# Fused linear attention and gated feed-forward layer: all row tails in the last block, batch 2's attention later in block 1, and half of batch 0's k^T v ahead of q's third turns

## The chip, the cores and the metric

The kernel runs on one core of a Trainium2 chip (trn2). The metric is the device time of one execution in microseconds (us); smaller is better. Five engines work on a core: PE (TensorE: matmuls and transposes by matmul, with a separate queue view PEld for its weight loads), DVE (VectorE), ACT (ScalarE), POOL (GpSimd) and SP (SyncE, which here only issues DMAs). POOL issues DMAs too.

## The reference

For 8 batches, 8 heads, 576 rows and a head size of 64, the attention is linear, with a cosine weight on the position; its output, with the heads side by side, is the input of a two-layer network:

```python
r = np.maximum(x, 0.0); phi(x) = np.concatenate([r * cos_w, r * sin_w], axis=-1)   # x: q or k
kv  = np.einsum('bhsf,bhsd->bhfd', k_p, v)
z   = np.sum(k_p, axis=2)
num = np.einsum('bhsf,bhfd->bhsd', q_p, kv)
den = np.einsum('bhsf,bhf->bhs', q_p, z)[..., None] + 1e-06
x   = (num / den).transpose(0, 2, 1, 3).reshape(4608, 512)
h   = x @ w_in                       # 512 x 2048
out = (h * sigmoid(1.702 * h)) @ w_out   # 2048 x 512
```

Inputs and output are float32; inside, matmuls take bf16 and add up in float32.

## The kernel before, in words

The order of all work is written out by hand: each engine runs its instructions in the order in which the program names them, and waits only for what it reads or overwrites. There is one block for each of the 8 batches. A block does the feed-forward layer of its batch and, in between, the attention of the next batch.

**Attention of a batch.** `trig` (lines 142 and 140) makes the weighted k (`kr`, nine slices of 64 rows, a cosine and a sine half each) on DVE, or on ACT with `act=True`. `vcopy` (lines 161 and 163) casts v to `vt`. For q there are two ways. In batches 0 and 1 `trig` makes nine slices `qn0`, `qturn_pe` (line 171) turns two slices at a time on PE and `qevac` (lines 179 and 181) copies them to `qT`. In batches 2 to 7 `trig_q` (line 155) and `qturn_dma` (line 189) do it in five chunks, the turn by a DMA that SP issues. `kv_mm` (line 207) is k^T v, 18 matmuls for each of four head pairs; `kv_evac` (line 212) copies it out of PSUM on DVE. `num_mm(c)` (line 230) is numerator and denominator of chunk c, that is 128 rows (chunk 4 has 64, the tail), `num_div` (lines 236, 238, 254) divides on DVE into `xn`. Then `xn` has to be turned: in batches 0 and 1 on PE (`xturn_mm`, line 272) with a copy on ACT (`xturn_evac`, line 279), in later batches by DMA (`xturn_dma`, line 285). `den_early` (line 244) makes the denominators of batch 0's first chunk ahead of its k^T v.

**Feed-forward.** The turned x of a batch has 512 columns, chunks 0 to 3, and a tail of 64 columns, chunk 4. `mm1(b, fc)` is four matmuls of 512 columns (line 295) for one of sixteen groups of 128 hidden units, with a Gelu on ACT (line 300). `mm2(b, t, lo, hi)` (line 345) is the second layer for row tile t of 128 rows over hidden groups lo to hi; when it is through, ACT copies it out (line 349), and a DMA stores it (line 352: POOL's queue, in the last block SP's).

**Tails.** Those of batches 0 and 1 are computed in their own blocks: `mm1_tail` (line 322) does 32 matmuls of 64 columns at a time, twice in a block, and a joint row tile `t == 4` of both batches goes through `mm2` in block 1. The tails of batches 2 to 7 wait in `xt` (384 columns); in the last block `mm1_tails` (line 313) does them with 16 x 4 matmuls of 384 columns, and three row tiles, 5 to 7, go through `mm2`.

**Order around the change.** At the start, batch 0: k is weighted, `ksum` makes z, q's slices are weighted on DVE, ACT and POOL as they land, PE turns them in pairs with some matmuls on a zero tile between them (`idle`, line 358), then come the two halves of k^T v with v from `vb`, which POOL's queue loads in two halves (line 132), and the first numerators. `start_block` (blocks 0 and 1) begins the first layer chunk by chunk, as x's chunks are turned. From block 1 on, DVE makes `trig_q`, `trig` and `vcopy` for the next batch while PE does the first layer; then PE does k^T v, and puts the numerators of the five chunks between half row tiles of the second layer. Behind the turns of x, SP issues the loads of k and v of the batch after (lines 562 to 564).

Of the kernel before, what the change touches and what calls it, by code (L numbers as in the profile page):

```python
# [19 lines left out]
def kernel(  # L20
# [9 lines left out]
    nc = tc.nc  # L30
# [80 lines left out]
    def w_in_of(kc, fc):  # L111
        return w_in_v[fc // 4][:, kc, fc % 4, :]
# [10 lines left out]
    def load_win(g):  # L123
        nc.gpsimd.dma_start(out=w_in_sb[g], in_=win_r[:, :, ts(g, 512)])
# [42 lines left out]
    def qturn_pe(c, home=None):  # L167
        tp = pmm.tile([128, 2, NI, 128], BF16, name="mm") if home is None else home
        for j in range(2 * c, min(2 * c + 2, NS)):
            for i in range(NI):  # L170
                nc.tensor.transpose(tp[:, j % 2, i], qn0[:, j, i, :], ident)  # L171
        tps[c] = tp
# [29 lines left out]
    def kv_mm(i0, i1, rhs, col, n):  # L202
        for i in range(i0, i1):
            for j in range(NS):
                for hh in range(2):
                    r = slice(hh * 64, hh * 64 + 64)
                    nc.tensor.matmul(st["kv", i][:, hh, ds(col, n)], kr[r, j, i, :], rhs(r, i, j),  # L207
                                     start=(j == 0), stop=(j == NS - 1))

    def kv_evac(i0, i1, n=65):  # L210
        o = st["kvs"][:, :, i0:i1, 0:n]
        nc.vector.tensor_copy(o, st["ps", i0].rearrange("p hh (i e) -> p hh i e", e=65)[:, :, :, 0:n])  # L212
# [13 lines left out]
    def num_mm(c):  # L226
        ps = pat.tile([128, 2, 512], F32, name="at")
        for h in range(H):
            i, hh = divmod(h, 2)
            nc.tensor.matmul(ps[:, h // 4, ds((h % 4) * 65, 65)], qT[:, h, ts(c, 128)],  # L230
                             st["kvs"][:, hh, i, 0:65], start=True, stop=True)
        nums[c] = [ps]
# [15 lines left out]
    def num_div(c, inv=None):  # L248
        ps = nums[c][0]
        pv = ps[:, :, 0:260].rearrange("p a (h e) -> p a h e", h=4)  # L250
        if inv is None:
            inv = inv_of(pv[:, :, :, 64])
        xn = small.tile([128, 2, 4, 64], BF16, name="xn", bufs=4)
        nc.vector.tensor_tensor(xn, pv[:, :, :, 0:64],  # L254
                                inv.unsqueeze(3).to_broadcast([128, 2, 4, 64]), op=MUL)
        nums[c].append(xn)

    x = {}

    TB = 2  # L260
    NT = (B - TB) * 64
    xt = one.tile([128, KC, NT], BF16, name="xt")

    def x_open(b):
        x[b] = xpool.tile([128, KC, S], BF16, name="xT")

    def xturn_mm(c):
        ps, xn = nums[c]
        xv = xn.rearrange("p a h e -> p (a h e)")
        for kc in range(KC):  # L270
            o = ps[:, kc // 2, ds(264 + (kc % 2) * 64, 64)].bitcast(BF16)
            nc.tensor.transpose(o, xv[:, ts(kc, 128)], ident)  # L272

    def xturn_evac(b, c):
        ps = nums.pop(c)[0]
        n = 128 if c < 4 else 64
        i = ps[:, :, 264:392].bitcast(BF16).rearrange("p a (k t) -> p a k t", k=2)[:, :, :, 0:n]
        o = x[b][:, :, c * 128:c * 128 + n].rearrange("p (a k) t -> p a k t", a=2)
        nc.scalar.activation(o, i, AF.Copy)  # L279

    def xturn_dma(b, c):
        xn = nums.pop(c)[1]
        n = 128 if c < 4 else 64
        o = xt[:, :, ts(b - TB, 64)] if c == 4 and b >= TB else x[b][:, :, c * 128:c * 128 + n]
        nc.sync.dma_start_transpose(out=o, in_=xn[0:n].rearrange("p a h e -> p (a h e)"))


    gT = {}
# [15 lines left out]
        mm1_part(b, fc, 0, MT)  # L304
        gelu(fc)

    gt = {}
    gl_t = one.tile([128, FC, NT], BF16, name="gl_t")

    def mm1_tails(fc):  # L310
# [2 lines left out]
            nc.tensor.matmul(hps, w_in_of(kc, fc), xt[:, kc, :], start=(kc == 0), stop=(kc == KC - 1))  # L313
        nc.scalar.activation(gl_t[:, fc, :], hps, AF.Gelu_apprx_sigmoid)  # L314

    def mm1_tail(b, half):
        if half == 0 and b % 2 == 0:
            gt[0] = gpool.tile([128, FC, 128], BF16, name="gtail", bufs=2)
        hps = pmm.tile([128, 8, 64], F32, name="mm")
        for f in range(8):  # L320
            for kc in range(KC):
                nc.tensor.matmul(hps[:, f], w_in_of(kc, half * 8 + f), x[b][:, kc, MT:S],  # L322
                                 start=(kc == 0), stop=(kc == KC - 1))
        nc.scalar.activation(gt[0][:, ts(half, 8), ts(b % 2, 64)], hps, AF.Gelu_apprx_sigmoid)

    yp = {}
    out_j = [out[b * S:b * S + S].rearrange("(p j) d -> j p d", j=NS) for b in range(2)]

    def rows(b, t):

        if t == 4:
            return [(64 * u, 64, out_j[u][NS - 1]) for u in range(2)]
        if t > 4:
            return [(64 * u, 64, out[(w + 1) * S - 64:(w + 1) * S])
                    for u, w in enumerate((TB + 2 * (t - 5), TB + 2 * (t - 5) + 1))]
        if b < 2:
            return [(64 * u, 64, out_j[b][2 * t + u]) for u in range(2)]
        return [(0, 128, out[b * S:b * S + 512].rearrange("(p c) d -> c p d", c=4)[t])]

    def mm2(b, t, lo, hi, c0=0, c1=d_model):  # L340
        if lo == 0:
            yp[t, c0] = pmm.tile([128, d_model], F32, name="mm")
        for fc in range(lo, hi):
            w = gT[fc][:, ts(t, 128)] if t < 4 else gt[0][:, fc, :] if t == 4 else gl_t[:, fc, ts(t - 5, 128)]
            nc.tensor.matmul(yp[t, c0][:, c0:c1], w, w_out_sb[:, fc, c0:c1],  # L345
                             start=(fc == 0), stop=(fc == FC - 1))
        if hi == FC:
            ysb = ypool.tile([128, d_model], F32, name="ysb")
            nc.scalar.activation(ysb[:, c0:c1], yp[t, c0][:, c0:c1], AF.Identity)  # L349
            for p0, n, dst in rows(b, t):  # L350
                eng = nc.sync if b == B - 1 else nc.gpsimd
                eng.dma_start(out=dst[:, c0:c1], in_=ysb[p0:p0 + n, c0:c1])  # L352
# [14 lines left out]
    def start_block(b, opened=False):  # L367

        if not opened:
            xturn_mm(0)  # L370
            xturn_evac(b, 0)
            num_mm(2)
            num_div(2)
            xturn_mm(1)
            xturn_evac(b, 1)
        for c in range(4):
            for fc in range(4):
                mm1_part(b, fc, c * 128, c * 128 + 128)
            if c == 0:
                num_mm(3)  # L380
                num_div(3)
                xturn_mm(2)
                xturn_evac(b, 2)
            if c == 1:
                num_mm(4)
                num_div(4)
                xturn_mm(3)
                xturn_evac(b, 3)
        for fc in range(4):
            gelu(fc)  # L390
        xturn_mm(4)
        mm1(b, 4)
        xturn_evac(b, 4)


    w = idle(12)
# [27 lines left out]
    nc.gpsimd.tensor_copy(gate[0:1, 1:2], vb[0:1, 3, 0:1])  # L424
    load_win(2)
    load_win(3)
    qturn_pe(2)
    for j in (6, 7):
        trig(qn0, qf0, j, act=True)
    qevac(0)  # L430
    qevac(1)
    qevac(2, act=True)
    kv_mm(0, 2, vb_rhs, 0, 64)
    inv0 = den_early(0)
    kv_evac(0, 2, 64)
    kv_mm(2, 4, vb_rhs, 0, 64)
# [22 lines left out]
        trig(kr, kf, j)  # L459
    for fc in range(5, FC):  # L460
        mm1(0, fc)
    mm1_tail(0, 0)
    mm1_tail(0, 1)
    for j in range(5):
        trig(qn0, qf0, j)
    for j in range(5, NS):
# [50 lines left out]
    for b in range(1, B):  # L517
        nb = b + 1 if b + 1 < B else None
        f0 = 5 if b == 1 else 0
        for fc in range(f0, FC):  # L520
            if nb is not None and fc == f0:
                for c in range(5):
                    trig_q(c)
                    qturn_dma(c)
                if nb + 1 < B:
                    load_q(nb + 1)
            if nb is not None and fc == f0 + 1:
                for j in range(NS):
                    trig(kr, kf, j)
                vcopy(0, 4)  # L530
            mm1(b, fc)
        if b < TB:
            mm1_tail(b, 0)
            mm1_tail(b, 1)
        if nb is None:
            for fc in range(FC):
                mm1_tails(fc)
            for t in (5, 6, 7):
                mm2(b, t, 0, FC)
            for t in range(3):  # L540
                mm2(b, t, 0, FC)
            mm2(b, 3, 0, FC, 0, 256)
            mm2(b, 3, 0, FC, 256, 512)
            continue
        x_open(nb)
        kv_open()
        kv_mm(0, 4, vt_rhs, 0, 65)
        kv_evac(0, 4)
        if b == 1:
            mm2(b, 4, 0, FC)  # L550
        for t in range(4):
            mm2(b, t, 0, 8)
            if t < 3:
                num_mm(2 * t)
                num_div(2 * t)
                xturn_dma(nb, 2 * t)
            mm2(b, t, 8, 16)
            if t < 2:
                num_mm(2 * t + 1)
                num_div(2 * t + 1)  # L560
                xturn_dma(nb, 2 * t + 1)
        if nb + 1 < B:
            load(kf, k, nb + 1, nc.sync)
            load(vf, v, nb + 1, nc.sync)
# [30 lines left out]
```

## Time and profile before

| | us |
|---|---|
| median of 3 runs | 293.15 (293.08 to 293.31) |
| the profiled execution, its own time | 293.47 |
| its span (first to last instruction) | 291.8 |
| PE busy | 286.0, 98% |
| DVE busy | 126.6, 43% |
| ACT busy | 130.4, 45% |
| PE's granted clock | 1.0 |

A profile page gives the busy time of each engine, the chain of work that ended last (followed back from the last instruction: at each step to what released it, or to the instruction before it on its engine) and groups of instructions by line. "PE at L207 x72" is 72 PE instructions of line 207 that write the tile "at". Timelines give start, length, engine, line and operation, and in brackets the idle time of the engine before it and what ended it. A waiting engine costs time only if others on the chain wait for it.

### The profile page before, as it was taken

The page shows a single profiled execution, that of the slowest core. Times are in us where ns is not written, and L with a number is a line of the kernel's source. Part 1 is how long each engine was busy: PE and PEld are TensorE (multiplying, and loading weights), DVE is VectorE, ACT ScalarE, POOL GpSimd, SP SyncE. Part 2 cuts the span into 40 slices and gives each one's busy share as a digit, 9 for nine tenths or more (in the row PEclk, how much of TensorE's full clock was granted, in tenths as well). Part 3 has the DMA queues.
Part 4 walks back from the last instruction along what each step waited for, and adds up shares of the span by engine and source line. Part 5 has one row for each costly group of instructions (what it writes and reads, how often), then busy time and mean ns, then how long its engine had stood idle before and what let it go on. Part 6 is the DMA issues. An engine that isn't in the chain of part 4 may idle for free.

```text
span 291.8 us, 6048 instructions
## 1 busy us (share of the span) xinstructions
PE 286.0 (98%) x2467; PEld 160.1 (55%) x2467; DVE 126.6 (43%) x364; ACT 130.4 (45%) x229; POOL 37.2 (13%) x70
## 2 busy tenths in 40 slices
PE   7999999999999999999999999999999999999995
PEld 3785656857545555555545554555455545565444
DVE  4864524791274636482658256625662420000000
ACT  7857743674115721472146313641265116773111
POOL 6650041400222001100110011001100010000000
PEclk9999999999999999999999999999999999999999
DMA  7999999595269966896579747995696341000322
GB/s 248 243 213 291 372 267 334 144 159 165 60 132 328 233 175 132 261 290 181 144 225 312 197 121 192 309 216 129 166 327 129 76 115 38 1 0 10 85 88 72
DMA packets 67227, 52.36 MB, mean 179 GB/s; under 512 B 47392, under 2 KB 57376, under 8 KB 67200
## 3 DMA queue, kind: packets, MB, share of 16 engines
q1 hardware_dynamic: 59824, 32.52, 44.5%
q0 software_dynamic: 7376, 19.47, 23.2%
q8 instruction: 19, 0.31, 0.4%
q14 instruction: 8, 0.07, 0.1%
HBM read 36.70 MB, written 9.44 MB: 158 GB/s over the span
## 4 chain that ended last, share of the span: by engine, by line
PE 95%; DMA 2%; DVE 1%; SPq 0%; ACT 0%; issue 0%; ACTq 0%
PE mm L345 43%; PE mm L295 38%; PE mm L313 4%; PE at L230 3%; PE at L207 3%; DMA qf<-in_q_dram 2%; PE mm L322 1%; PE at L272 1%; PE at L171 1%; DVE qn L142 1%; PE mm L171 0%; SPq L62 0%; ACT xT L279 0%; SPq L63 0%; PE mm L358 0%
## 5 line engine op out<-in xcount | busy, mean ns | idle before, releaser
L345 PE MATMUL mm<-w_out_sb,g 128*128 128x512 bf16 (+1 forms) x528 | 117.7, 372 | 0.0
L295 PE MATMUL mm<-xT,w_in 128*128 128x512 bf16 (+1 forms) x608 | 113.2, 345 | 0.0
L300 ACT ACTIVATE g<-mm 128x512 bf16<-128x512 f32 x128 | 75.7, 599 | 31.8 <-PE mm L295 31.8
L295 PEld LDWEIGHTS <-w_in 128*128 128x128 bf16 x608 | 62.0, 114 | 49.1
L345 PEld LDWEIGHTS <-g 128*128 128x128 bf16 x528 | 48.7, 98 | 49.5
L349 ACT ACTIVATE ysb<-mm 128x512 f32<-128x512 f32 (+1 forms) x37 | 21.7, 586 | 111.4 <-PE mm L345 111.4
L352 POOL DMA_DIRECT2D out_dram<-ysb x38 | 20.7, 547 | 177.1 <-ACT ysb L349 177.0
L142 DVE TENSOR_SCALAR kr<-kf,cosw 128x256 bf16<-128x256 f32 x68 | 23.7, 349 | 30.2 <-DMA kf<-in_k_dram 30.2
L254 DVE TENSOR_TENSOR xn<-at,inv 128x512 bf16<-128x512 f32 x40 | 27.7, 691 | 1.7 <-PE at L230 0.4
L142 DVE TENSOR_SCALAR kr<-kf,sinw 128x256 bf16<-128x256 f32 x68 | 23.9, 351 | 0.0
L236 DVE TENSOR_SCALAR den<-at 128x8 f32<-128x8 f32 x39 | 6.5, 166 | 36.5 <-PE at L230 36.5
L230 PEld LDWEIGHTS <-qT 128*128 128x128 bf16 x320 | 14.6, 97 | 8.1 <-issue 0.8
L212 DVE CAST kvs<-at 128x520 bf16<-128x520 f32 (+1 forms) x9 | 5.7, 635 | 29.1 <-PE at L207 29.1
L230 PE MATMUL at<-kvs,qT 128*128 128x65 bf16 x320 | 15.9, 193 | 0.7 <-ACT xT L279 0.7
L155 DVE TENSOR_SCALAR qn<-qf,sinw 128x512 bf16<-128x512 f32 (+1 forms) x30 | 14.3, 478 | 0.0
L155 DVE TENSOR_SCALAR qn<-qf,cosw 128x512 bf16<-128x512 f32 (+1 forms) x30 | 14.3, 477 | 0.0
L313 PE MATMUL mm<-xt,w_in 128*128 128x384 bf16 x64 | 10.6, 326 | 0.0
L345 PE MATMUL mm<-w_out_sb,gl_t 128*128 128x512 bf16 x48 | 10.5, 379 | 0.0
L207 PEld LDWEIGHTS <-kr 64*128 64x128 bf16 x576 | 9.2, 94 | 2.3 <-issue 2.0
L358 PE MATMUL mm<-warm 128*128 128x512 bf16 x23 | 8.6, 494 | 1.2 <-DVE warm L76 1.2
L313 PEld LDWEIGHTS <-w_in 128*128 128x128 bf16 x64 | 7.2, 113 | 3.3
L314 ACT ACTIVATE gl_t<-mm 128x384 bf16<-128x384 f32 x16 | 7.9, 491 | 2.4 <-PE mm L313 2.4
(68 smaller groups left out, 126.4 us busy)
## 6 DMA issues: line engine op xcount, KB each, us to landing
kf<-in_k_dram SPq DMA_DIRECT2D x5, 1152.0 KB, 6.7
vf<-in_v_dram SPq DMA_DIRECT2D x5, 1152.0 KB, 9.7
qf<-in_q_dram SPq DMA_DIRECT2D x5, 1024.0 KB, 6.1
out_dram<-ysb POOLq DMA_DIRECT2D x20, 256.0 KB, 2.6
kf<-in_k_dram POOLq DMA_DIRECT2D x2, 1152.0 KB, 10.6
vf<-in_v_dram POOLq DMA_DIRECT2D x2, 1152.0 KB, 14.4
out_dram<-ysb POOLq DMA_DIRECT2D x18, 128.0 KB, 3.1
w_in<-in_moe_w_in_dram POOLq DMA_DIRECT2D x4, 512.0 KB, 9.3
```

What stands on the lines that cost most here:

```text
L142: eng.tensor_scalar(o, i, 0.0, w[:, j:j + 1], op0=MAX, op1=MUL)
L155: nc.vector.tensor_scalar(o, i, 0.0, sc, op0=MAX, op1=MUL)
L207: nc.tensor.matmul(st["kv", i][:, hh, ds(col, n)], kr[r, j, i, :], rhs(r, i, j), start=(j == 0), stop=(j == NS - 1))
L230: nc.tensor.matmul(ps[:, h // 4, ds((h % 4) * 65, 65)], qT[:, h, ts(c, 128)], st["kvs"][:, hh, i, 0:65], start=True, stop=True)
L254: nc.vector.tensor_tensor(xn, pv[:, :, :, 0:64], inv.unsqueeze(3).to_broadcast([128, 2, 4, 64]), op=MUL)
L295: nc.tensor.matmul(hp[fc][:, t0:t1], w_in_of(kc, fc), x[b][:, kc, t0:t1], start=(kc == 0), stop=(kc == KC - 1))
L300: nc.scalar.activation(g, hp.pop(fc), AF.Gelu_apprx_sigmoid)
L313: nc.tensor.matmul(hps, w_in_of(kc, fc), xt[:, kc, :], start=(kc == 0), stop=(kc == KC - 1))
L345: nc.tensor.matmul(yp[t, c0][:, c0:c1], w, w_out_sb[:, fc, c0:c1], start=(fc == 0), stop=(fc == FC - 1))
L349: nc.scalar.activation(ysb[:, c0:c1], yp[t, c0][:, c0:c1], AF.Identity)
L352: eng.dma_start(out=dst[:, c0:c1], in_=ysb[p0:p0 + n, c0:c1])
L358: nc.tensor.matmul(w, warm[:, 0:128], warm, start=True, stop=True)
```

## The change

1. The tails of batches 0 and 1 join `xt`, which has 512 columns now (`NT = B * 64`); `mm1_tail` is gone, `mm1_tails` works on 512 columns, and four row tiles, 4 to 7, go through `mm2` in the last block. The tail chunk of batches 0 and 1 is turned by DMA (`xturn_dma(b, 4)`) and no longer on PE.
2. `start_block` has another order of its last first-layer parts: three hidden groups of chunk 2, two of chunk 3, the fourth of chunk 2, the other two of chunk 3.
3. In block 1, four of the nine k slices of batch 2 and half of its v copy go to ACT, between and behind the Gelus. k^T v and all that follows of batch 2's attention stand half a row tile of the second layer later (`lag`). In the blocks from 2 on, the rewritten loop gives the order of before.
4. In batch 0, `kv_mm(0, 2)` stands ahead of `qturn_pe(2)` and no longer behind it.

```diff
--- before.py
+++ after.py
@@ -257,12 +257,14 @@
 
     x = {}
 
-    TB = 2
-    NT = (B - TB) * 64
+    NT = B * 64
     xt = one.tile([128, KC, NT], BF16, name="xt")
 
     def x_open(b):
-        x[b] = xpool.tile([128, KC, S], BF16, name="xT")
+        x[b] = xpool.tile([128, KC, MT], BF16, name="xT")
+
+    def x_of(b, c):
+        return xt[:, :, ts(b, 64)] if c == 4 else x[b][:, :, ts(c, 128)]
 
     def xturn_mm(c):
         ps, xn = nums[c]
@@ -273,16 +275,14 @@
 
     def xturn_evac(b, c):
         ps = nums.pop(c)[0]
-        n = 128 if c < 4 else 64
-        i = ps[:, :, 264:392].bitcast(BF16).rearrange("p a (k t) -> p a k t", k=2)[:, :, :, 0:n]
-        o = x[b][:, :, c * 128:c * 128 + n].rearrange("p (a k) t -> p a k t", a=2)
+        i = ps[:, :, 264:392].bitcast(BF16).rearrange("p a (k t) -> p a k t", k=2)
+        o = x_of(b, c).rearrange("p (a k) t -> p a k t", a=2)
         nc.scalar.activation(o, i, AF.Copy)
 
     def xturn_dma(b, c):
         xn = nums.pop(c)[1]
         n = 128 if c < 4 else 64
-        o = xt[:, :, ts(b - TB, 64)] if c == 4 and b >= TB else x[b][:, :, c * 128:c * 128 + n]
-        nc.sync.dma_start_transpose(out=o, in_=xn[0:n].rearrange("p a h e -> p (a h e)"))
+        nc.sync.dma_start_transpose(out=x_of(b, c), in_=xn[0:n].rearrange("p a h e -> p (a h e)"))
 
 
     gT = {}
@@ -304,7 +304,6 @@
         mm1_part(b, fc, 0, MT)
         gelu(fc)
 
-    gt = {}
     gl_t = one.tile([128, FC, NT], BF16, name="gl_t")
 
     def mm1_tails(fc):
@@ -313,26 +312,14 @@
             nc.tensor.matmul(hps, w_in_of(kc, fc), xt[:, kc, :], start=(kc == 0), stop=(kc == KC - 1))
         nc.scalar.activation(gl_t[:, fc, :], hps, AF.Gelu_apprx_sigmoid)
 
-    def mm1_tail(b, half):
-        if half == 0 and b % 2 == 0:
-            gt[0] = gpool.tile([128, FC, 128], BF16, name="gtail", bufs=2)
-        hps = pmm.tile([128, 8, 64], F32, name="mm")
-        for f in range(8):
-            for kc in range(KC):
-                nc.tensor.matmul(hps[:, f], w_in_of(kc, half * 8 + f), x[b][:, kc, MT:S],
-                                 start=(kc == 0), stop=(kc == KC - 1))
-        nc.scalar.activation(gt[0][:, ts(half, 8), ts(b % 2, 64)], hps, AF.Gelu_apprx_sigmoid)
-
     yp = {}
     out_j = [out[b * S:b * S + S].rearrange("(p j) d -> j p d", j=NS) for b in range(2)]
 
     def rows(b, t):
 
-        if t == 4:
-            return [(64 * u, 64, out_j[u][NS - 1]) for u in range(2)]
-        if t > 4:
-            return [(64 * u, 64, out[(w + 1) * S - 64:(w + 1) * S])
-                    for u, w in enumerate((TB + 2 * (t - 5), TB + 2 * (t - 5) + 1))]
+        if t >= 4:
+            return [(64 * u, 64, out_j[w][NS - 1] if w < 2 else out[(w + 1) * S - 64:(w + 1) * S])
+                    for u, w in enumerate((2 * (t - 4), 2 * (t - 4) + 1))]
         if b < 2:
             return [(64 * u, 64, out_j[b][2 * t + u]) for u in range(2)]
         return [(0, 128, out[b * S:b * S + 512].rearrange("(p c) d -> c p d", c=4)[t])]
@@ -341,7 +328,7 @@
         if lo == 0:
             yp[t, c0] = pmm.tile([128, d_model], F32, name="mm")
         for fc in range(lo, hi):
-            w = gT[fc][:, ts(t, 128)] if t < 4 else gt[0][:, fc, :] if t == 4 else gl_t[:, fc, ts(t - 5, 128)]
+            w = gT[fc][:, ts(t, 128)] if t < 4 else gl_t[:, fc, ts(t - 4, 128)]
             nc.tensor.matmul(yp[t, c0][:, c0:c1], w, w_out_sb[:, fc, c0:c1],
                              start=(fc == 0), stop=(fc == FC - 1))
         if hi == FC:
@@ -373,24 +360,24 @@
             num_div(2)
             xturn_mm(1)
             xturn_evac(b, 1)
-        for c in range(4):
-            for fc in range(4):
+        def part(c, *fcs):
+            for fc in fcs:
                 mm1_part(b, fc, c * 128, c * 128 + 128)
-            if c == 0:
-                num_mm(3)
-                num_div(3)
-                xturn_mm(2)
-                xturn_evac(b, 2)
-            if c == 1:
-                num_mm(4)
-                num_div(4)
-                xturn_mm(3)
-                xturn_evac(b, 3)
+
+        for c in range(2):
+            part(c, 0, 1, 2, 3)
+            num_mm(c + 3)
+            num_div(c + 3)
+            xturn_mm(c + 2)
+            xturn_evac(b, c + 2)
+        xturn_dma(b, 4)
+        part(2, 0, 1, 2)
+        part(3, 0, 1)
+        part(2, 3)
+        part(3, 2, 3)
         for fc in range(4):
             gelu(fc)
-        xturn_mm(4)
         mm1(b, 4)
-        xturn_evac(b, 4)
 
 
     w = idle(12)
@@ -424,13 +411,13 @@
     nc.gpsimd.tensor_copy(gate[0:1, 1:2], vb[0:1, 3, 0:1])
     load_win(2)
     load_win(3)
+    kv_mm(0, 2, vb_rhs, 0, 64)
     qturn_pe(2)
     for j in (6, 7):
         trig(qn0, qf0, j, act=True)
     qevac(0)
     qevac(1)
     qevac(2, act=True)
-    kv_mm(0, 2, vb_rhs, 0, 64)
     inv0 = den_early(0)
     kv_evac(0, 2, 64)
     kv_mm(2, 4, vb_rhs, 0, 64)
@@ -459,8 +446,6 @@
         trig(kr, kf, j)
     for fc in range(5, FC):
         mm1(0, fc)
-    mm1_tail(0, 0)
-    mm1_tail(0, 1)
     for j in range(5):
         trig(qn0, qf0, j)
     for j in range(5, NS):
@@ -525,17 +510,18 @@
                 if nb + 1 < B:
                     load_q(nb + 1)
             if nb is not None and fc == f0 + 1:
-                for j in range(NS):
+                for j in range(NS if b > 1 else 5):
                     trig(kr, kf, j)
-                vcopy(0, 4)
+                vcopy(0, 4 if b > 1 else 2)
             mm1(b, fc)
-        if b < TB:
-            mm1_tail(b, 0)
-            mm1_tail(b, 1)
+            if b == 1 and fc in (7, 9, 11, 13):
+                trig(kr, kf, (fc + 3) // 2, act=True)
+        if b == 1:
+            vcopy(2, 4, act=True)
         if nb is None:
             for fc in range(FC):
                 mm1_tails(fc)
-            for t in (5, 6, 7):
+            for t in (4, 5, 6, 7):
                 mm2(b, t, 0, FC)
             for t in range(3):
                 mm2(b, t, 0, FC)
@@ -543,22 +529,17 @@
             mm2(b, 3, 0, FC, 256, 512)
             continue
         x_open(nb)
-        kv_open()
-        kv_mm(0, 4, vt_rhs, 0, 65)
-        kv_evac(0, 4)
-        if b == 1:
-            mm2(b, 4, 0, FC)
-        for t in range(4):
-            mm2(b, t, 0, 8)
-            if t < 3:
-                num_mm(2 * t)
-                num_div(2 * t)
-                xturn_dma(nb, 2 * t)
-            mm2(b, t, 8, 16)
-            if t < 2:
-                num_mm(2 * t + 1)
-                num_div(2 * t + 1)
-                xturn_dma(nb, 2 * t + 1)
+        lag = 1 if b == 1 else 0
+        for u in range(8):
+            if u == lag:
+                kv_open()
+                kv_mm(0, 4, vt_rhs, 0, 65)
+                kv_evac(0, 4)
+            if 0 <= u - lag - 1 < 5:
+                num_mm(u - lag - 1)
+                num_div(u - lag - 1)
+                xturn_dma(nb, u - lag - 1)
+            mm2(b, u // 2, 8 * (u % 2), 8 * (u % 2) + 8)
         if nb + 1 < B:
             load(kf, k, nb + 1, nc.sync)
             load(vf, v, nb + 1, nc.sync)
```

## The prediction

> **What bounds the kernel now.** I read the page's busy line first, then the chain of waits, then the chain in order of time, and only for single places the timelines of the engines and the DMA rows.
>
> ```profile
> span 291.8 us, 6048 instructions
> PE 286.0 (98%) x2467; PEld 160.1 (55%) x2467; DVE 126.6 (43%) x364; ACT 130.4 (45%) x229; POOL 37.2 (13%) x70
> ...
> PE 95%; DMA 2%; DVE 1%; SPq 0%; ACT 0%; issue 0%; ACTq 0%
> ```
>
> PE has work in 98% of the span and is 95% of the chain that ended last; DVE, ACT and the queues are on it only in the first microseconds. So what the change does to the time is what it takes from PE's instruction stream, less any new wait of PE, plus what it does to the start. A busy PE is a modelled thing, therefore the terms below are taken from the chain, whose pieces follow each other start to start.
>
> **The tails.** The chain in order of time shows (start, length, what) both removed stretches (line 322), a PE turn (line 272), a middle block's first layer (line 295) and the work of the last block that grows (line 313):
>
> ```profile
> 21.07 0.22 PE at L272 x4
> ...
> 31.65 2.13 PE mm L322 x64
> 33.78 5.18 PE mm L345 x24
> 38.96 0.89 PE at L171 x16
> ...
> 67.48 2.13 PE mm L322 x64
> ...
> 89.39 13.81 PE mm L295 x64
> 103.20 1.19 PE at L207 x72
> ...
> 253.88 10.40 PE mm L313 x64
> ```
>
> Removed: two stretches of 64 matmuls of 64 columns, 2 x 2.13 = 4.26 us (33.3 ns each). Also removed: the PE turn of the tail chunk in batches 0 and 1, two times four transposes, 2 x 0.22 = 0.44 us. Added: the 64 tail matmuls of the last block take 512 columns and not 384. At 384 they cost 10.40 / 64 = 162.5 ns; 64 matmuls of 512 columns cost 13.81 us in every middle block, 215.8 ns each. That is 13.81 - 10.40 = 3.41 us more. The sixteen second-layer matmuls of the joint tail of batches 0 and 1 only move, from block 1 to the last block: nothing for PE, and their output goes out through SP's queue before seven other row tiles. PE's sum is -4.26 - 0.44 + 3.41 = -1.29 us.
>
> The Trainium skill (TensorE: Matmul & The Clock Gate, section Back-to-back issue gap) speaks against this: its table gives a matmul of up to 64 columns about 60 cycles, 25 ns at full clock. By that the removal would be worth an estimated 3.2 us and the tails alone would lose 0.2 us. The trace does not agree: 33.3 ns each, in both stretches alike.
>
> **The start.** Before, PE stood waiting for the third pair of q's slices, and the first half of k^T v came behind it:
>
> ```profile
> 9.86 0.49 ACT L140 ACTIVATE qn<-qf,sinw 128x256 bf16<-128x256 f32 x1
> ```
>
> ```profile
> 11.11 1.27 DVE L181 COPY qT<-mm 128x1024 bf16<-128x1024 bf16 x2
> 12.60 0.17 DVE L236 TENSOR_SCALAR den<-mm 128x8 f32<-128x8 f32 x1 [0.22 <-PE mm L244]
> ...
> 12.92 0.75 DVE L212 CAST kvs<-at 128x256 bf16<-128x256 f32 x2
> ```
>
> ```profile
> 11.24 0.40 PE mm L171 x4
> 11.64 0.64 PE at L207 x36
> 12.28 0.28 PE mm L244 x8
> ...
> 13.75 0.49 PE at L230 x16
> ```
>
> ```profile
> L132 POOL DMA_DIRECT2D vb<-in_v_dram x2: 758/838/917, 4.4 to 5.3; - x2
> ...
> DMA to landing us min/median/max: 6.3/6.5/6.8
> ```
>
> After the change: the second group of turns has its data when ACT ends at 9.86 + 0.49 = 10.35, and four transposes (0.22) later PE is free, about 10.6. The first half of v lands at 4.4 + 6.3 = 10.7, so the first half of k^T v runs 10.75 to 11.4. The eight turns of the third group (0.44) end at 11.85; the first DVE copy is then done (about half of 1.27 behind 11.11, 11.8), so the denominators end at 12.13. The second half of v lands at 5.3 + 6.8 = 12.1: second half of k^T v to 12.8, eight turns to 13.3. DVE no longer idles its 0.22, so its copies of k^T v end at 13.67 - 0.22 = 13.45. The numerators' second four heads, which before began at 13.75 + 0.12, now begin at 13.5: 0.37 gained. I take 0.35, because v lands exactly when it is wanted; the ends are 0.1 (both halves of v 0.3 later) and 0.45 (PE alone: 13.75 - 13.3). A loss would need v later than 11.6, which its row does not bear out.
>
> **Batches 0 and 1: the turn by DMA.** SP's queue has nothing to do at that time, so the two DMA turns hold up no one there. They do take DMA time while batch 1's loads run, and PE wants q of batch 1 earlier. Its 16 transposes stood at 38.96 and now come 0.35 + 0.22 + 2.13 = 2.70 us sooner, at 36.26, the fourth slice at 36.9.
>
> ```profile
> 35.48 0.34 DVE L142 TENSOR_SCALAR qn<-qf,sinw 128x256 bf16<-128x256 f32 x1
> ```
>
> ```profile
> 60.00:62.00 2.00, 2.00 (x11) 1.08 (x10) 2.00 (x9) 1.47 (x3) 0.00 (x0) 1.00 1.70 160
> ```
>
> The fourth slice was ready at 35.48 + 0.34 = 35.82, so q may land 1.1 us later for nothing. In the window from 60 to 62 us, in which turns are nearly all of the traffic, 160 GB/s (the last column) went with a DMA share of 1.70 (the column before it), 94 GB/s at a share of one; 64 rows of 1 KB cost the engines 0.7 us by that. It fits: cost 0, and 1 us per us if that cover is gone.
>
> The new order of the parts (three of chunk 2, then chunk 3) comes to chunk 3 after 12 matmuls instead of 16:
>
> ```profile
> 19.28 1.79 PE mm L295 x32
> ```
>
> ```profile
> 19.32 0.60 ACT L279 ACTIVATE xT<-at 128x512 bf16<-128x512 bf16 x1 [0.79 <-PE at L272]
> ```
>
> 12 x 1.79 / 32 = 0.67: PE arrives at 19.95, ACT's copy ends at 19.92. A wait of 0.02 at most in each of the two blocks; left out.
>
> **Block 1.** DVE gives four of nine k slices and half of the v copy to ACT.
>
> ```profile
> L300 ACT ACTIVATE g<-mm 128x512 bf16<-128x512 f32 x128 | 75.7, 599 | 31.8 <-PE mm L295 31.8
> ...
> L161 ACT ACTIVATE vt<-vf 128x1152 bf16<-128x1152 f32 x1 | 1.2, 1160 | 0.0
> ```
>
> ```profile
> 64.62 1.34 DVE L163 CAST vt<-vf 128x2304 bf16<-128x2304 f32 x1
> ```
>
> Eleven Gelus, eight k halves (0.49 each, as the q slice at 9.86 above) and the copy are 11 x 0.6 + 8 x 0.49 + 1.16 = 11.7 us even with nothing overlapped. PE's eleven first-layer groups take 11 x 0.863 = 9.5, then half a row tile 1.73, and the third k^T v pair (the first that reads ACT's half of v) comes 0.6 later: 11.8. So ACT just fits, and behind the copy only the next output copy is queued. DVE, done at 65.96 before, has 4 x 2 x 0.26 + 0.6 = 2.7 us less to do, as much as PE comes earlier. Cost 0.
>
> Batch 2's attention stands half a row tile later, so its turned x has less time before block 2, whose first matmuls want chunks 0 to 3:
>
> ```profile
> 83.43 1.59 SPq L285 DMA_TRANSPOSE xT<-xn  x1
> ```
>
> ```profile
> xT<-xn SPq DMA_TRANSPOSE x1, 3.5
> ```
>
> ```profile
> DMA to landing us min/median/max: 2.3/2.5/4.5
> ```
>
> Chunk 3's turn was issued at 83.43 and landed at 86.9; block 2 began at 89.39: 2.5 us to spare, now 2.5 - 1.73 = 0.7. With the largest landing of all turns, 4.5, PE would wait 0.3. I take 0. On SP behind these turns stand k and v of batch 3, also 1.73 later against block 2:
>
> ```profile
> 98.03 1.36 DVE L163 CAST vt<-vf 128x2304 bf16<-128x2304 f32 x1
> ```
>
> DVE ended at 99.4 for a k^T v at 103.20; 3.8 less 1.73 leaves 2.1. Nothing.
>
> **Sum.** -1.29 - 0.35 = -1.64 us. The profiled execution took 293.47 (span 291.8 and 1.67 around it), so 291.83 by it; the median of the runs, 293.15, lies 0.32 lower: 291.5.
>
> **Rivals.**
> (a) The start gives nothing: v lands a little later than in this one execution, or DVE's chain holds what PE wins. For it: the two times agree to 0.1 us. Against it: DVE's own idle 0.22 goes too. 293.15 - 1.29 = 291.9. Chance 0.12.
> (b) A short wait at block 2 for chunk 3, 0.3 us by the largest landing, or as much for ACT's half of v: 291.8, at twice that 292.1. Chance 0.08.
> (c) The narrow matmuls are dear only because PE waits there. At the wide ones' rate 64 columns cost 215.8 / 8 = 27 ns, 128 of them 3.45, and the tails would gain 0.04 and not 0.85: -0.83, 292.3. Against it: both stretches last 2.13 to the digit, without a wait in the chain. By the page's 25 ns it would be an estimated 292.6. Chance 0.05.
> (d) Slower: chunk 3's turn meets a load in SP's ring. In block 2 a turn issued right behind k and v had this row:
>
> ```profile
> qT<-qn SPq DMA_TRANSPOSE x1, 10.0
> ```
>
> With 10.0 for chunk 3 and 4.2 us from its issue to block 2, PE would stand 5.8 us: 297.3. It turns slower than before once the landing passes 4.2 + 1.64 = 5.8 us. It decides if q of batch 3, issued before these turns, is still moving when they are issued; it should have landed some 2 us ahead. Chance 0.05.
> That the change does not do what it says is ruled out by the built order of instructions, in which the narrow matmuls are gone and k^T v stands ahead.
>
> **How the numbers follow.** 0.70 for the forecast, 291.5, whose own range from the ends of the start's gain and 0.1 for the small waits is 291.3 to 291.9. Two runs of this kernel can be told apart by about 0.2%, 0.59 us: faster means below 292.56. Forecast, (a) and (b) make 0.90 faster; (c), at that edge, is the 0.05 of the same; (d) is the 0.05 slower. The range 291.1 to 292.3 goes 0.2 below the forecast's own for the scatter of a median and up to (c).
>
> **What would show it.** Right: no row of 64-column matmuls, the tail group 13.8 us and not 10.4, batch 0's first numerators near 13.4 and not 13.75, block 2 beginning 8.5 us earlier (4.26 + 0.44 + 0.35, and 16 x 0.216 = 3.45 for the moved tail matmuls, at the 5.18 / 24 of the row at 33.78) without a wait. Wrong: a PE wait for xT at block 2's first matmul (b, d), PE waiting for vb near 10.7 or 12.1 (a), for qn near 36.3, or for kr or vt in block 1.

## The result, and the profile after

The changed kernel takes 292.53 us (median of 13 runs, 292.36 to 292.76) against 293.29 (13 runs, 293.06 to 293.48): ratio 0.9975, 95% interval 0.9967 to 0.9984. It is faster, by 0.76 us and not by the 1.64 of the sum; the time lies above the predicted range. The profiled execution took 292.54, with a span of 290.8. The ratios, here and below, take in all executions of both kernels and lie close to the ratios of the means, not of the medians; the intervals of the experiments are 0.5 to 0.8 us wide. Some executions of the experiments took 0.5 to 0.9 us longer than the rest, and no trace shows one of those, so differences of a few tenths are read from the chains.

The page of the changed kernel:

```profile
span 290.8 us, 5790 instructions
PE 284.3 (98%) x2331; PEld 155.1 (53%) x2331; DVE 124.0 (43%) x356; ACT 132.9 (46%) x232; POOL 35.9 (12%) x68
...
PE 96%; DMA 2%; ACT 0%; DVE 0%; SPq 0%; issue 0%; ACTq 0%
```

Its chain in order of time (start, length, what), at the places of the prediction:

```profile
12.90 0.55 PE mm L171 x8
13.45 0.49 PE at L230 x16
...
18.72 0.23 PE at L274 x4
18.95 0.67 PE mm L295 x12
19.62 0.01 issue
19.63 11.64 PE mm L295 x68
31.27 5.18 PE mm L332 x24
...
53.27 0.01 issue
53.29 11.64 PE mm L295 x68
64.93 1.73 PE mm L332 x8
66.65 1.19 PE at L207 x72
...
77.80 3.45 PE mm L332 x16
81.25 13.81 PE mm L295 x64
...
245.75 13.81 PE mm L312 x64
...
287.31 0.38 ACT ysb L336
```

The narrow matmuls are gone, the tail group is 13.81 to the digit, the first numerators stand at 13.45 and not 13.75, and block 2 begins at 81.25 without a wait. But it begins 89.39 - 81.25 = 8.14 us earlier and not 8.5. And there is a break behind the first 12 of the 80 matmuls of line 295 in blocks 0 and 1, where before 32 ran without one, up to the turn. The span behind the last copy has grown, too. Before, the chain ended so, in a span of 291.8:

```profile
288.58 0.38 ACT ysb L349
```

That is 3.2 us ahead of the end. Now it is 290.8 - 287.31 = 3.5.

Two theories came from this. **A**: the PE turn of the tail chunk was worth nothing, because PE turned while it would otherwise have waited; without it PE waits 0.18 us in each of blocks 0 and 1, first for x's chunk 3. **B**: the end is longer because the last store's DMA semaphore now stands earlier in the row in which SP checks them. The rival to both was that these are chances of one execution, or that the new order of the parts costs by itself.

### The profile page after: what moved, and what is told of

The parts are those of the page before. It is cut to its first block, busy times and chain, and to the rows that moved or that the text cites. A ratio compares the mean times of both kernels' runs of the same rounds, so it can differ in the third digit from the quotient of the medians.

```text
span 290.8 us, 5790 instructions
## 1 busy us (share of the span) xinstructions
PE 284.3 (98%) x2331; PEld 155.1 (53%) x2331; DVE 124.0 (43%) x356; ACT 132.9 (46%) x232; POOL 35.9 (12%) x68
## 4 chain that ended last, share of the span: by engine, by line
PE 96%; DMA 2%; ACT 0%; DVE 0%; SPq 0%; issue 0%; ACTq 0%
PE mm L332 43%; PE mm L295 38%; PE mm L312 5%; PE at L230 3%; PE at L207 3%; DMA kf<-in_k_dram 2%; PE mm L171 1%; PE mm L345 1%; PE at L171 1%; PE at L274 1%; DVE kr L142 0%; PE mm L218 0%; ACT xT L280 0%; SPq L62 0%; ACT ysb L336 0%
## 5 line engine op out<-in xcount | busy, mean ns | idle before, releaser
L339 POOL DMA_DIRECT2D out_dram<-ysb x36 | 19.4, 540 | 172.9 <-ACT ysb L336 171.1
L142 DVE TENSOR_SCALAR kr<-kf,cosw 128x256 bf16<-128x256 f32 x64 | 22.8, 357 | 30.7 <-DMA kf<-in_k_dram 30.7
L142 DVE TENSOR_SCALAR kr<-kf,sinw 128x256 bf16<-128x256 f32 x64 | 22.1, 345 | 0.0
L230 PEld LDWEIGHTS <-qT 128*128 128x128 bf16 x320 | 14.6, 97 | 8.1 <-issue 0.8
L312 PE MATMUL mm<-xt,w_in 128*128 128x512 bf16 x64 | 14.0, 379 | 0.0
L332 PE MATMUL mm<-w_out_sb,gl_t 128*128 128x512 bf16 x64 | 14.0, 379 | 0.0
L313 ACT ACTIVATE gl_t<-mm 128x512 bf16<-128x512 f32 x16 | 9.6, 597 | 4.2 <-PE mm L312 4.2
L332 PEld LDWEIGHTS <-gl_t 128*128 128x128 bf16 x64 | 6.2, 98 | 7.6
```

Source lines behind the costliest of these rows:

```text
L142: eng.tensor_scalar(o, i, 0.0, w[:, j:j + 1], op0=MAX, op1=MUL)
```

## The experiments

### Old order of the last parts

```diff
-        part(2, 0, 1, 2)
-        part(3, 0, 1)
-        part(2, 3)
-        part(3, 2, 3)
+        part(2, 0, 1, 2, 3)
+        part(3, 0, 1, 2, 3)
```

> The changed kernel with the old order of start_block's last parts (four hidden groups of chunk 2, then four of chunk 3). Theory A: in the changed kernel PE waits 0.18 us in each of blocks 0 and 1 for ACT's copy of x's chunk 3; with four more matmuls ahead of chunk 3 (4 x 0.056 = 0.22) that wait goes, but the first Gelu begins 0.05 later against PE's last part and, with no PE turn left there, PE then waits about 0.17 for the Gelu's PSUM tile before the fifth hidden group. So no change: 292.5, within 0.1, and the gap of PE stands at another place. Rival: the new order itself loses the 0.36 us of the two gaps and the old one gives them back: 292.2.

Measured: 292.55 us (292.43 to 293.42, 11 runs), ratio to the kernel before 0.9982 (0.9973 to 0.999): as the changed kernel. Its chain:

```profile
18.88 1.79 PE mm L295 x32
20.67 0.01 issue
20.68 10.52 PE mm L295 x48
```

The wait in front of chunk 3 is gone: 32 matmuls run in 1.79. It stands in front of the fifth hidden group instead: 48 matmuls of 512 columns take 10.52 where they took 10.36. From the first part of chunk 2 to the second layer it is 1.79 + 0.01 + 10.52 = 12.32, and 0.67 + 0.01 + 11.64 = 12.32 in the changed kernel. The trace's events give both waits their causes. PE starts a matmul of 128 columns every 0.056 us. In the changed kernel one start, the first for chunk 3, comes 0.234 behind the one before it, at 19.63; ACT's copy of chunk 3 ended at 19.58. Here the same 0.234 stands ahead of the fifth hidden group, at 20.69; the matmul waits for ACT, whose first Gelu ended at 20.63. The order only moves the wait. Theory A holds, the rival falls, by the profiled execution (292.47): five of the eleven took over 293.0, and their traces are not known.

### The tail chunk turned on PE again

```diff
...
-        xturn_dma(b, 4)
...
         for fc in range(4):
             gelu(fc)
+        xturn_mm(4)
         mm1(b, 4)
+        xturn_evac(b, 4)
```

It also has the old order of the parts; the copy goes into `xt`.

> The changed kernel with the tail chunk of batches 0 and 1 turned on PE again (and copied by ACT, now into the joint tail tile) and with the old order of start_block's last parts. The prediction's step: taking the two PE turns away is worth 0.44, so this is 0.44 slower than the changed kernel: 293.0. Theory A: PE would only wait there otherwise, so bringing the turns back costs 0.1 at most: 292.6. Two DMAs fewer on SP move the last semaphore two places back, so by theory B 0.12 us are gained at the end: 292.5.

Measured: 292.89 us (292.46 to 293.44, 11 runs), ratio 0.9983 (0.9973 to 0.9994). The runs scatter too widely to tell 292.6 from 293.0; the chain of the profiled execution (292.60) does:

```profile
18.84 1.79 PE mm L296 x32
20.62 0.22 PE at L274 x4
20.85 10.36 PE mm L296 x48
```

1.79 + 0.22 + 10.36 = 12.37 with the turn, 12.32 without it, in block 1 as in block 0. Taking 0.22 us of work from PE here makes the stretch 0.05 shorter. The first experiment is this kernel without the turn: its median is 0.34 lower, but the ratios, 0.9982 and 0.9983, and the profiled executions, 292.47 and 292.60, do not bear out the prediction's 0.44. The other half of the expectation failed: SP has two DMAs fewer than in the changed kernel, but the end did not get shorter (last copy at 287.33, span 290.9). The semaphores go round in eights, as the run with four stores fewer shows below: two back from the fourth place is the second, which is worse, and not a place nearer the end.

### Chunk 3's copy on DVE

```diff
...
             num_mm(c + 3)
-            num_div(c + 3)
+            if c == 0:
+                num_div(c + 3)
             xturn_mm(c + 2)
-            xturn_evac(b, c + 2)
+            xturn_evac(b, c + 2, dve=c == 1)
+            if c == 1:
+                num_div(c + 3)
```

> The changed kernel, but in start_block the turned chunk 3 of x is copied out of PSUM by DVE, ahead of the division of chunk 4, instead of by ACT. Theory A: a DVE copy of this size takes about 0.42 instead of ACT's 0.60, so chunk 3 is there 0.18 us sooner and both gaps of 0.18 close: 292.53 - 0.36 = 292.2. Rival: the gap is not ACT's copy but the first Gelu's length (PE waits elsewhere as soon as this wait goes): 292.5.

Measured: 292.41 us (292.35 to 292.45, 6 runs), ratio 0.997 (0.9958 to 0.9982): 0.12 less than the changed kernel and not 0.36. ACT's copy in the timeline of the changed kernel, then DVE's copy and a PEld row in the timelines of this one, and this one's chain:

```profile
18.98 0.60 ACT L280 ACTIVATE xT<-at 128x512 bf16<-128x512 bf16 x1 [0.77 <-PE at L274]
```

```profile
19.19 0.42 DVE L281 COPY xT<-at 128x512 bf16<-128x512 bf16 x1 [0.49 <-PE at L274]
```

```profile
16.21 0.87 PEld L298 LDWEIGHTS <-w_in 128*128 128x128 bf16 x15 [0.35 <-DMA w_in<-in_moe_w_in_dram]
```

```profile
19.16 12.15 PE mm L298 x80
```

The copy takes 0.42 and not 0.60, and the stretch is 12.15 without a break, 0.17 less, in block 1 too. But block 0 had already lost 0.2: the first first-layer matmul waited for the first part of w_in, which landed at 16.2 us in this execution and between 14.6 and 15.0 in the nine other traces. So theory A's wait is closed, and in block 0 of this execution the time was given back ahead of it. The edit is not the cause of the late landing: the last experiment has it too, and w_in landed at 14.7 there. All six times lie within 0.1 us of each other, so w_in may have been late in all of them; only one has a trace.

### Four stores fewer on SP

```diff
-                eng = nc.sync if b == B - 1 else nc.gpsimd
+                eng = nc.sync if b == B - 1 and t not in (4, 5) else nc.gpsimd
```

> The changed kernel, but in the last block the stores of the first two tail row tiles (four DMAs) go through POOL's queue, so that SP issues four DMAs fewer. Theory B: at the end SP waits for the DMA semaphores one after the other, 0.06 us each; the last store's semaphore is the fourth in that row in the changed kernel and the eighth before, so four more checks stand behind the last landing. Four DMAs fewer put it back to the eighth place: 292.53 - 0.24 = 292.3, and the span behind the last ACT copy is 3.26 us as before and not 3.52. Rival: the end's 0.26 us is the landing of the last store, not the order of semaphores: 292.5.

Measured: 292.24 us (292.12 to 292.43, 5 runs), ratio 0.9964 (0.9952 to 0.9977), 0.29 less than the changed kernel. SP's waits at the end, first of the changed kernel, then of this one, and four rows of this one's chain:

```profile
SPq L571 <- DMA out_dram<-ysb: 1.4, 1, 1.4
```

```profile
SPq L571 <- DMA out_dram<-ysb: 1.0, 1, 1.0
```

```profile
10.94 0.04 issue
10.98 0.71 PE at L207 x36
...
13.66 0.48 PE at L230 x16
...
287.51 0.38 ACT ysb L336
```

The last copy begins at 287.51 in a span of 290.7: 3.2 us, as before the change. (That the copy begins 0.20 later than in the changed kernel has nothing to do with the stores: in this execution the first half of v landed at 10.94, PE waited 0.2 us for it, and the numerators began at 13.66.) The trace's events of SP say why the end is short again. After the last store it checks the DMA semaphores in a fixed order, one every 0.06 us, and stands still at the one that the last store raises:

```
the changed kernel       four stores fewer       (start in us, semaphore)
288.10  S114             288.30  S114
288.17  S101             288.37  S101
288.23  S103             288.43  S103
289.64  S104  <- last    288.50  S104
289.70  S105             288.56  S105
289.76  S115             288.62  S115
289.82  S116             288.68  S116
289.88  S117             289.75  S117  <- last
289.94  S118             289.82  S118
290.00  drain            289.88  drain
```

SP's DMAs take the semaphores in turn. The change gives SP four more (two turns, two stores), and the last store moves from S117 to S104: four checks now stand behind the landing instead of being over by then, 0.25 us. The whole end is 0.33 longer, 3.52 against 3.19 by the trace's events, and the other 0.08 is the rival's: the last store's semaphore was raised 1.90 us behind its issue in the changed kernel, and 1.81 to 1.82 both here and before. Theory B holds for three quarters of it.

### Batch 0's k^T v back behind q's third turns

```diff
-    kv_mm(0, 2, vb_rhs, 0, 64)
     qturn_pe(2)
...
     qevac(2, act=True)
+    kv_mm(0, 2, vb_rhs, 0, 64)
     inv0 = den_early(0)
```

> The changed kernel with the first half of batch 0's k^T v behind q's third turns again, as before. The prediction's step: that order is worth 0.35 us, so 292.9, with PE idle about 0.4 ahead of the third group's last four turns, as in the trace of before. Rival: what is won there is given back at the first first-layer matmul, which waits for the first part of w_in (it landed at 16.2 us in one execution), so 292.5.

Measured: 292.79 us (292.54 to 293.24, 11 runs), ratio 0.9983 (0.9974 to 0.9993): 0.26 more than the changed kernel. Its chain:

```profile
11.14 0.40 PE mm L171 x4
...
13.65 0.49 PE at L230 x16
```

The numerators begin at 13.65, 0.20 later than in the changed kernel, and 0.10 earlier than in the profiled execution of before with the same order. PE's idle time ahead of the third group's last four turns is back, 0.25 us by the starts of its matmuls, and nothing is given back at w_in, so the rival falls. In PE's timelines of all ten profiled executions the numerators begin between 13.1 and 13.5 with the new order (seven) and between 13.4 and 13.6 with the old one (three); the means are 0.2 apart. So the new order is worth 0.2 to 0.26 in the mean, and nothing in an execution in which v lands late, as in the run with four stores fewer; the profiled one of before stood on the long side.

### Block 1 as it was

```diff
-                for j in range(NS if b > 1 else 5):
+                for j in range(NS):
                     trig(kr, kf, j)
-                vcopy(0, 4 if b > 1 else 2)
+                vcopy(0, 4)
             mm1(b, fc)
-            if b == 1 and fc in (7, 9, 11, 13):
-                trig(kr, kf, (fc + 3) // 2, act=True)
-        if b == 1:
-            vcopy(2, 4, act=True)
...
-        lag = 1 if b == 1 else 0
+        lag = 0
```

> The changed kernel without the changes of block 1: all nine k slices and the whole v copy of batch 2 on DVE, and batch 2's attention ahead of the first half row tile. The prediction's step: these changes cost nothing; from the trace, DVE would end its copy of v at 53.3 + 4.0 + 4.7 + 1.4 = 63.4 us and PE comes to k^T v at 64.8, so leaving them out costs nothing either: 292.5, no wait of PE for kr or vt. Rival: with the tails gone from block 1 PE comes to k^T v ahead of DVE, and the move was needed: PE waits there and the time is over 293.0.

Measured: 292.64 us (292.53 to 293.26, 11 runs), ratio 0.9975 (0.9966 to 0.9984). DVE's last row ahead of k^T v, and the chain:

```profile
62.09 1.34 DVE L163 CAST vt<-vf 128x2304 bf16<-128x2304 f32 x1
```

```profile
53.26 11.64 PE mm L295 x68
64.90 1.19 PE at L207 x72
```

DVE is through at 63.4, PE comes at 64.9 and does not wait. The later attention and ACT's share neither cost nor gain anything that can be measured; the rival, that they were needed, falls.

### The joint tails alone

This is the kernel before with the first edit of the change only: the tails of all batches go to the last block (`NT = B * 64`), but PE still turns them. Block 1, batch 0's start and the order of the parts are those of before.

> The kernel before with the joint tails alone: the tails of batches 0 and 1 go to the last block, but are turned on PE and copied by ACT, the parts have the old order, block 1's attention and batch 0's k^T v stand as before. PE's sum: 4.26 away, 3.41 more. By the prediction's term alone 293.3 - 0.85 = 292.4. By theory B the last store's semaphore comes to the second place of SP's row (two DMAs more), 0.37 later at the end: 292.8. Rival: the narrow matmuls were dear because PE waited there, and the tails gain 0.04: 293.3 or more.

Measured: 292.78 us (292.61 to 293.59, 11 runs), ratio 0.9979 (0.9969 to 0.9988). The expected 292.8 had the tails' 0.85 less the 0.37 of the end. Its chain:

```profile
13.55 0.49 PE at L230 x16
...
287.51 0.38 ACT ysb L337
```

From the first numerators to the last copy it is 273.96 us, and 288.58 - 13.75 = 274.83 before: 0.87 less. The last copy begins 3.6 us ahead of the end of the span (291.1): the last store's semaphore is the second in the row. That the narrow matmuls were dear only because PE waited there is ruled out, also by the trace of before, in which they start 0.033 us apart one after the other.

### All three waits closed

Chunk 3's copy by DVE as above, and:

```diff
-                eng = nc.sync if b == B - 1 else nc.gpsimd
+                eng = nc.sync if b == B - 1 and t != 4 and (t, p0) != (5, 0) else nc.gpsimd
...
         for c in range(2):
-            part(c, 0, 1, 2, 3)
+            early = opened and c == 0
+            part(c, 0, 1, 2)
+            if not early:
+                part(c, 3)
             num_mm(c + 3)
+            if c == 0:
+                num_div(c + 3)
+            if early:
+                part(c, 3)
...
```

> The changed kernel with three further edits: chunk 3's copy by DVE (as in the run with that alone), three of the first tail stores of the last block through POOL's queue, so that the last store's semaphore becomes the last but none of SP's row, and in block 1 the numerators of chunk 3 ahead of the fourth hidden group of chunk 0, where PE waits 0.18 us for a PSUM tile. By theories A and B: 0.36 (0.12 in the run alone) + 0.31 + 0.18, that is 291.7 to 291.9. Rival: waits that are closed open at the next place (w_in's landing in block 0, the Gelu's tile in block 1): only the end's 0.31 is left, 292.2.

Measured: 291.81 us (291.65 to 292.13, 5 runs), ratio 0.9948 (0.9935 to 0.9961). It lies in the expected range and below both kernels. Its chain:

```profile
18.99 12.15 PE mm L298 x80
...
49.54 0.67 PE mm L298 x12
50.21 0.24 PE at L230 x8
50.45 0.23 PE mm L298 x4
```

Both stretches of blocks 0 and 1 run through, the numerators fill the place where PE waited for a PSUM tile at 50.3, and the span (289.9) ends 3.1 us behind the last copy (286.80). From trace to trace (291.65 against 292.54) it is 0.89 us less than the changed kernel: 2 x 0.17 in the stretches, 0.17 at the tile and 0.38 at the end.

## Why the prediction was wrong, point by point

**The direction and the mechanism** were right: PE is the bound, and what leaves its stream shortens the time where nothing else takes the place.

**The tails**, -0.85: right. The tail group measured 13.81, and the kernel with the joint tails alone came out where this term and the end put it (0.87 by its chain). The 25 ns that the table of the Trainium skill gives a matmul of up to 64 columns (TensorE: Matmul & The Clock Gate, Back-to-back issue gap) did not hold for this stream of weight loads and matmuls; the 33.3 ns of the row did.

**The PE turns**, -0.44: this step failed. What came was 2 x 0.05, from 12.37 to 12.32 in each block. The prediction looked at the wait for chunk 3 and put it at 0.02, by an error in reading. It took PE's arrival from the chain, 19.28 + 0.67 = 19.95, and ACT's end, 19.92, from a timeline. But the chain does not run "start to start": it sets its pieces by the matmuls' ends, and those are modelled. PE's timeline of before has the same parts earlier:

```profile
19.12 1.95 PE L295 MATMUL mm<-xT,w_in 128*128 128x128 bf16 x32
```

By it PE arrives at 19.12 + 0.67 = 19.79 and waits till 19.96 (ACT's end, and the 0.04 to 0.05 that PE took to go on in the traces): 0.17 in each block, 0.35 of the 0.44. The other question, what the turn had covered, was not asked. The old order would have waited as long for the Gelu's PSUM tile, as the first experiment shows.

**The start**, -0.35: mis-sized. 0.30 in the two profiled executions, 0.26 by the times and 0.20 by the trace when that edit is undone. Its mechanism held: PE is no longer idle ahead of the third turns, and DVE's 0.22 of idle time is gone. But the prediction gave eight turns behind k^T v 0.44 us; the chain above has 0.55, and so PE came to the numerators at 13.45 and not at 13.3.

**The end**, put at nothing in the sum: +0.33, of which four checks are 0.25. "Their output goes out through SP's queue" was noted and costed at nothing, because the stores are early. What counted was their number, not their time.

**The profiled execution**: it stood 0.18 above the later median of before (293.29). That median in turn is 0.14 above the 293.15 of three runs from which the forecast was taken, so 0.14 of the miss is the starting point's. The traces' spans differ by 0.9 to 1.0, the medians by 0.76.

Together: -0.85 - 0.10 - 0.30 + 0.33 = -0.92 from trace to trace, where 292.54 - 293.47 = -0.93 was measured. Less the 0.18 of that last point it is 0.74, against 0.76 by the medians.

**Block 1 and the DMA turns**, 0: right. No wait at block 2, for kr or vt, or for q of batch 1. Chunk 3's DMA turn in block 1 was issued at 77.0 and landed in 2.4 us, 1.8 ahead of block 2 and not 0.7, so neither (b) nor (d) came; not (c), see the tails alone. Rival (a) did not come in the changed kernel's trace, in which PE stood some 0.03 us for v; it came in that of the run with four stores fewer, in which v landed 0.2 us later. The two terms that failed most lay outside the rivals, at a place that the prediction had costed at 0.02 and at one that it had not costed. One estimate has no ground: 94 GB/s came from a share of 1.70, and a share above one is no share of time in which the engines were busy; in the first half of that window 182 GB/s went with a share of 1.00. The 0.7 us worked out from it was covered in any case.

## What to carry to other kernels

Before work is taken from the bounding engine, ask at that very place what it would do in that time: here a turn of 0.22 us between a chain of copies and the next full tile cost 0.05. Compare arrival and readiness only on one clock, the starts of the timelines, and keep the chain for lengths. Count a change's DMAs by queue, because the number alone can move the last store in the order in which the program's end is checked.

## What the runs showed of the hardware that was not expected

SP's checks at the end come every 0.06 us in a fixed order, and the DMAs of its queue go round eight semaphores, so that the place of the last one was worth up to 0.4 us: 3.1 us from the last copy to the end in the best kernel, 3.6 with the joint tails alone. In the five traces in which the last store has S104, that semaphore is raised 1.89 to 1.90 us behind the issue, and 1.81 to 1.82 in the five others, with S101, S117 or S118; why is open. The early DMA turn in block 0, beside the loads of batch 1, took long without harm:

```profile
DMA to landing us min/median/max: 2.4/5.7/9.1
```

These are the two early turns of `xt`: 9.1 us in block 0, 2.4 in block 1. The first part of w_in landed 8.5 to 8.8 us after its issue in nine traces and 10.1 in one, which was enough for PE to wait; why is open.
